# Chunk attention and cosine router: the weight copies at a change of expert move from ScalarE to GpSimd

## The chip, the cores and the metric

The kernel runs on one core of one Trainium2 chip. The metric is device time in microseconds of one execution; where several runs are shown, their median. The profile is of one execution, taken by the hardware profiler, and has its own time.

## The reference

Attention in chunks of 64 rows feeds a mixture of experts in which each token goes to one expert of eight.

```python
# attention, B = 8, H = 8, S = 576, D = 64, in chunks of 64 rows
scores = scale * np.matmul(q_c, k_c.transpose(0, 1, 2, 4, 3))
attn = softmax(scores)
out = np.matmul(attn, v_c)              # x = out as (4608, 512)
# router and experts, E = 8, w1 (8, 512, 1024), w2 (8, 1024, 512)
expert_idx = np.argmax(logits, axis=1)
for e in range(E):
    mask = expert_idx == e
    h = np.maximum(x[mask] @ w1[e], 0.0)
    out[mask] = gate_w[mask, None] * (h @ w2[e])
```
All data are float32.

## The kernel before

The first part, up to about 180 us, computes the attention and the router and scatters the token rows, ordered by expert, into a DRAM buffer. The second part, with which this document deals, goes through these rows in steps. A step j takes 128 token rows in two halves of 64, s = 0 and s = 1; each half belongs to one expert, half 0 going up through the experts from the first, half 1 coming down from the last. Each half has its own weights in SBUF: `w1_sb[s]`, `w2_sb[s]` in two buffers, and `next_w1[s]`, into which the w1 of the half's next expert is loaded well ahead (`load_behind`, L177).

From step 3 on, `hidden_fast` computes the hidden layer with seven block products in place of eight (Strassen's method). The w1 of a half is cut in four blocks B11, B12, B21, B22; four combinations T1 to T4 of them are made by VectorE in `add_up` (L291), T1, T2 and T4 into `sums`, T3 in the place of B12. The inputs have combinations S of their own (`add_x`, L318, four VectorE instructions of 128x128 with both inputs in SBUF). On TensorE the products (L342) come in the order p1 (B11), p2 (B21), p3 (B22), p5 (T1), p6 (T2), p7 (T3), p4 (T4), 16 matmuls each with both halves in turn, in six PSUM banks used round and round; so p4 has the bank of the same step's p1. Behind p4 stands `result` of the step before: 64 matmuls with w2 (L413) into one of two PSUM tiles.

The order on every engine is written out by hand (`manual_schedule`), so each engine's queue follows the source:

- ScalarE, in `hidden_fast`: the copy U of p1 out of PSUM (L377), square root and exponent for the gates (L224, L231, each with a table load), relu of c11, c12 and c22 (L361), then `swap_next`, then relu of the last block, then the scaling y of the finished result (L421).
- VectorE: c11 = U + p2, `turn_xb` and `add_x` for the next step (L203, L318), the sums for c12 and c22 (L374), then `swap_next`, the last block U - p4 (L374), and two transposes into hT (L368).
- GpSimd: one indirect DMA per step that scatters y to the output (L428). It waits for y.
- SyncE: the loads of rows, of w2 and of `next_w1`.

`swap_next` calls `take_next`. For each half it reads one number of `swap` into a register of the engines named (L137) and branches on it (L299, "tc.If"). If the half's expert changes, three quarters of w1 are copied from `next_w1` to `w1_sb` (L301), 1024 elements on each of 128 partitions per copy, and `add_up` makes T1 to T4 from `next_w1` (four VectorE instructions). If not, the engine adds to its semaphore what the skipped instructions would have added, and goes on. The next step's p1, p2 and p3 wait for these copies' semaphore in either case.

```python
p1 = product(x[:, 0, 0], "B11")
nc.scalar.copy(U, p1)
...
relu(1, 1, c22)
p4 = product(x[:, 1, 1], "T4")
swap_next()
add(U, U, p4, ALU.subtract)
relu(1, 0, U)
```

Of the kernel before, what the change touches and what calls it, by code (L numbers as in the profile page):

```python
# [16 lines left out]
ENG = mybir.EngineType  # L17
# [8 lines left out]
def kernel(  # L26
# [11 lines left out]
    nc = tc.nc  # L38
# [69 lines left out]
    swap = keep.tile([P, NST], I32, name="swap")  # L108
# [3 lines left out]
    def of_step(s, j):  # L112
        c = NST - 1 - (j - NE)
        return slice(G * s, G * s + 1), slice(c, c + 1)
# [21 lines left out]
    def number(ap, top, *engines):  # L136
        return nc.values_load(  # L137
            ap,
            engines=engines,
            min_val=0,  # L140
            max_val=top,
            skip_runtime_bounds_check_because="a count of comparisons, less than this",
        )
# [132 lines left out]
    def block(s, m, w1=None):  # L276

        if m in TS:
            return sums_sb[s][:, TS.index(m)]
        u, v = UV[m]  # L280
        return (w1 or w1_sb)[s].rearrange("p (u c) (v x) -> p u v c x", u=2, v=2)[:, u, v]

    def add_up(s, w1, which):
        for o, a, b in (
            ("T1", "B12", "B11"),
            ("T2", "B22", "T1"),
            ("T3", "B22", "B12"),
            ("T4", "T2", "B21"),
        ):
            if o in which:  # L290
                nc.vector.tensor_tensor(  # L291
                    block(s, o), block(s, a, w1), block(s, b, w1), ALU.subtract
                )

    def take_next(j):

        for s in range(2):
            f = number(swap[of_step(s, j)], 1, ENG.DVE, ENG.Activation)
            with tc.If(f > 0):  # L299
                for m in ("B11", "B21", "B22"):  # L300
                    nc.scalar.copy(block(s, m), block(s, m, next_w1))  # L301
                add_up(s, next_w1, ("T1", "T2", "T3", "T4"))

    def quarters(xT):
# [808 lines left out]
    next_w1 = [late_p.tile([P, KD, F], FP32, name=f"next_w1_{s}") for s in range(2)]  # L1113
# [6 lines left out]
    with (  # L1120
# [18 lines left out]
        for j in range(LEAST - 1):  # L1139
# [9 lines left out]
            def swap_next():  # L1149
                if NE <= n < LEAST:  # L1150
                    take_next(n)
# [93 lines left out]
```

## Time and profile before

| what | value |
|---|---|
| three runs | median 676.58 us (675.12 to 679.66) |
| the profiled execution | 675.66 us |
| its span | 673.8 us |
| mean granted TensorE clock | 0.988 |
| ScalarE, L301 copies | 18, mean 1044 ns |
| VectorE, L291 subtractions at a change | 24, mean 1218 to 1226 ns |
| VectorE, L318 | 132, mean 292 ns |
| GpSimd, L428 scatters of whole rows | 36, mean 1002 ns |
| loads of swap (L137) on ScalarE | 64, median 453 ns |
| loads of swap on VectorE | 64, median 524 ns |

The span runs from the first to the last instruction of the program on the core; what lies around it is start and end of the execution. In the views, a row of a group has the line, the engine, the operation, the tiles out<-in and the shape, then busy time and mean duration, then the engine's idle time ahead of it and what ended that. In the timeline a row begins with its start and duration in us, and ends with the idle time ahead of it and its releaser. PEld is TensorE's weight load, and a q after an engine's name is its sequencer.

### The profile page before, as it was taken

To read this page: it belongs to the slowest core of one execution; us is meant where nothing else is said; L and a number is where in the kernel's file an instruction comes from. 1 tells how busy PE (TensorE), PEld (TensorE's weight loads), DVE (VectorE), ACT (ScalarE), POOL (GpSimd) and SP (SyncE) were. 2 spreads that over 40 slices of the span, in tenths; PEclk is the share of its full clock that TensorE was granted. 3 is DMA by queue.
4 is the path that set the end of the run, shared out by engine and by line. 5 is a ranking of instruction groups with operands and counts; after the bars stand their busy time and mean duration, and the time that the engine had idled before them with its cause. 6 is when DMAs were issued, how large, how long until landed. Compare 5 with 4: busy or idle time off the path is not lost. (4 is left out here: it accounts for less than half of the span.)

```text
span 673.8 us, 24854 instructions
## 1 busy us (share of the span) xinstructions
PE 628.7 (93%) x9744; PEld 366.8 (54%) x9744; DVE 420.9 (62%) x1140; ACT 445.8 (66%) x776; POOL 158.4 (24%) x237
## 2 busy tenths in 40 slices
PE   5989999999789999999999999999999999999993
PEld 4867777776446667667434444334444444444441
DVE  3848888887469555656575466767654666564430
ACT  4746667666124777677877867778777777877650
POOL 6738887743311000000100100001001000100101
PEclk9979999999989999999999999999999999999998
DMA  9998899989918711112777111776821114411101
GB/s 249 235 246 235 240 293 267 266 231 348 363 54 302 279 51 46 43 40 71 293 262 282 57 37 48 281 281 228 330 70 44 44 48 162 172 43 34 51 28 37
DMA packets 94686, 112.66 MB, mean 167 GB/s; under 512 B 52460, under 2 KB 72684, under 8 KB 94552
## 3 DMA queue, kind: packets, MB, share of 16 engines
q1 hardware_dynamic: 82824, 72.84, 33.8%
q0 software_dynamic: 11696, 38.04, 17.1%
q8 instruction: 81, 1.33, 0.8%
q14 instruction: 53, 0.43, 0.2%
q10 hardware_dynamic: 32, 0.02, 0.0%
HBM read 334.71 MB, written 22.69 MB: 530 GB/s over the span
## 5 line engine op out<-in xcount | busy, mean ns | idle before, releaser
L413 PE MATMUL y_ps<-w,hT 128*32 128x512 f32 (+1 forms) x2368 | 272.6, 589 | 0.0
L361 ACT ACTIVATE h<-C 64x256 f32<-64x256 f32 x264 | 178.6, 677 | 95.5 <-DVE C L374 68.9
L413 PEld LDWEIGHTS y_ps<-w,hT 128*32 128x32 f32 x2368 | 103.3, 110 | 142.3 <-issue 110.2
L428 POOL DMA_INDIRECT out_dram<-y,spot x36 | 36.1, 1002 | 436.9 <-ACT y L421 208.8
L374 DVE TENSOR_TENSOR C<-C,h 128x256 f32<-128x256 f32 x231 | 96.1, 416 | 49.2 <-DVEq L299 42.5
L342 PE MATMUL h<-w,S 128*32 128x256 f32 x1056 | 95.6, 379 | 0.0
L342 PE MATMUL h<-sums,xbT 128*32 128x256 f32 x1056 | 94.8, 379 | 0.0
L342 PE MATMUL h<-w,xbT 128*32 128x256 f32 x1056 | 78.5, 380 | 7.1 <-ACTq L299 6.0
L368 DVE STREAM_TRANSPOSE hT<-h 128x512 f32<-128x512 f32 x66 | 46.7, 708 | 44.1 <-ACT h L361 44.0
L342 PEld LDWEIGHTS h<-w,xbT 128*32 128x32 f32 x1056 | 43.0, 110 | 39.8 <-ACTq L299 13.4
L342 PEld LDWEIGHTS h<-w,S 128*32 128x32 f32 x1056 | 50.4, 110 | 20.3 <-ACT w L301 0.4
L342 PEld LDWEIGHTS h<-sums,xbT 128*32 128x32 f32 x1056 | 50.0, 110 | 20.3 <-ACT C L377 0.6
L227 DVE TENSOR_SCALAR rn<-rn 128x1 f32<-128x1 f32 x37 | 5.7, 153 | 68.9 <-ACT rn L224 68.9
L342 PE MATMUL h<-sums,S 128*32 128x256 f32 x528 | 47.8, 379 | 0.0
L813 POOL DMA_INDIRECT spots<-xr,dest x36 | 37.4, 1039 | 30.3 <-DVE dest L778 9.0
L203 DVE STREAM_TRANSPOSE xbT<-xin 128x256 f32<-128x256 f32 x73 | 44.2, 643 | 0.5 <-DVE hT L368 0.5
L224 ACT ACT_TABLE_LOAD x34 | 43.6, 1283 | 0.9 <-issue 0.3
L231 ACT ACT_TABLE_LOAD x34 | 43.6, 1283 | 0.6
L421 ACT ACTIVATE y<-y_ps,gate 128x512 f32<-128x512 f32 (+1 forms) x37 | 25.2, 682 | 24.1 <-issue 8.8
L695 ACT COPY xT<-tr 128x512 f32<-128x512 f32 x36 | 21.1, 586 | 29.8 <-PE tr L693 25.4
L585 POOL DMA_DIRECT2D kx<-in_k_dram x36 | 32.0, 891 | 19.7 <-PE tr L608 18.8
L585 POOL DMA_DIRECT2D qx<-in_q_dram x40 | 34.5, 866 | 1.6 <-PE tr L608 0.8
(202 smaller groups left out, 807.9 us busy)
## 6 DMA issues: line engine op xcount, KB each, us to landing
w<-in_moe_w_dram SPq DMA_DIRECT2D x74, 2048.0 KB
next_w<-in_moe_w_dram SPq DMA_DIRECT2D x67, 2048.0 KB
xin<-spots SPq DMA_DIRECT2D x158, 64.0 KB
qx<-in_q_dram POOLq DMA_DIRECT2D x32, 256.0 KB
v<-in_v_dram SPq DMA_DIRECT2D x56, 144.0 KB
kx<-in_k_dram POOLq DMA_DIRECT2D x28, 256.0 KB
spots<-blank SPq DMA_DIRECT2D x9, 144.0 KB
spot<-spots SPq DMA_DIRECT2D x80, 4.0 KB
```

The lines of the kernel that those rows point to most:

```text
L203: nc.vector.transpose(xT[:, :, cols].rearrange("p c (b i) -> p b c i", i=Q), t[:, s * (D // 2) : (s + 1) * (D // 2)].rearrange("p (b i c) ...
L224: nc.scalar.activation(rn, spot[:, j % SPOTS, SQ : SQ + 1], AF.Sqrt)
L231: nc.scalar.activation(sh, sh, AF.Exp, accum_out=gate)
L342: nc.tensor.matmul(ps[t0 : t0 + Q], lhsT=a[:, c, s], rhs=w[:, r], start=c == 0, stop=c == KD // 2 - 1,)
L361: nc.scalar.activation(h[b][G * v : G * v + G, s].rearrange("p (k i) -> p k i", i=Q), x[G * s : G * s + G].rearrange("p (i k) -> p k i", i=Q),
L368: nc.vector.transpose(hT.rearrange("p k (s b i) -> p b s k i", b=2, i=Q)[:, b], h[b].rearrange("p s (k i) -> p s k i", i=Q),)
L374: nc.vector.tensor_tensor(out, a, b, op)
L413: nc.tensor.matmul(ps[Q * r : Q * r + Q, 0:w], lhsT=d["hT"][:, c, Q * t0 : Q * t0 + Q], rhs=w2_sb[s][buf_of(j)][:, c, d0 : d0 + w], start= ...
L421: nc.scalar.activation(y[:, 0:w], ps[:, 0:w], AF.Copy, scale=gate_of.pop(j))
L428: ins = nc.gpsimd.indirect_dma_start(out=to, out_offset=bass.IndirectOffsetOnAxis(ap=at, axis=0), in_=y[:, 0:w], in_offset=None, bounds_ch ...
L585: eng.dma_start(out=x[done : done + n], in_=src[b, :, s : s + n, :].rearrange("h p d -> p h d"),)
L813: ins = nc.gpsimd.indirect_dma_start(out=spots, out_offset=bass.IndirectOffsetOnAxis(ap=at, axis=0), in_=m, in_offset=None, bounds_check=S ...
```

## The change

In `take_next`, GpSimd in place of ScalarE reads `swap`, branches on it, and makes the three copies. ScalarE has no conditional left in these steps. The instructions of TensorE and VectorE are the same in number and order. On GpSimd the two tests and the copies stand between the scatter of one result and the scatter of the next.

```diff
     def take_next(j):
 
         for s in range(2):
-            f = number(swap[of_step(s, j)], 1, ENG.DVE, ENG.Activation)
+            f = number(swap[of_step(s, j)], 1, ENG.DVE, ENG.Pool)
             with tc.If(f > 0):
                 for m in ("B11", "B21", "B22"):
-                    nc.scalar.copy(block(s, m), block(s, m, next_w1))
+                    nc.gpsimd.tensor_copy(block(s, m), block(s, m, next_w1))
                 add_up(s, next_w1, ("T1", "T2", "T3", "T4"))
```

## The prediction

> **What bounds the kernel now.** I read the page's busy times first, then what the matmuls wait for from 250 us to the end (the waits view of PE), then the groups by form of ACT and POOL, and last the timeline around an expert change.
>
> ```profile
> PE 628.7 (93%) x9744; PEld 366.8 (54%) x9744; DVE 420.9 (62%) x1140; ACT 445.8 (66%) x776; POOL 158.4 (24%) x237
> ```
> ```profile
> PE h L342 <- ACTq L299: 6.0, 7, 1.3
> PE h L342 <- ACT w L301: 0.9, 1, 0.9
> ```
> TensorE is the bound, and in the stage concerned the matmuls wait for nothing but ScalarE's conditional (L299 is the If; "ACTq" is ScalarE's sequencer) and its copies. So the change touches the only thing TensorE waits for there. How much that is worth is read from the step starts. I call T the start of a step's first product p1 (B11). In the PE timeline undisturbed steps are 12.91 us apart (302.26 to 315.17). Three stretches are longer: T goes from 302.26 to 370.52 in 5 steps (3.71 us too long), from 409.25 to 492.88 in 6 (6.17) and from 544.51 to 584.14 in 3 (0.90). **10.8 us** in all, more than the 6.9 us of the waits view because an undisturbed p1 overlaps the product before it by 0.57 us. These stretches hold the expert changes: the source view of L301 has 18 copies, three to a half, so six changes; the 64 tests of L299 on ScalarE have 58 skips, which agrees. From the timeline they lie in the steps with T = 302.26 (half 1), 329.67 (half 0), 409.25 (half 0), 422.16 (half 1), 451.83 (half 0), 544.51 (half 0).
>
> ```profile
> 302.26 2.08 PE L342 MATMUL h<-w,xbT 128*32 128x256 f32 x31
> 303.80 0.37 ACT L377 COPY C<-h 128x256 f32<-128x256 f32 x1 [0.18 <-PE h L342]
> 303.89 0.98 POOL L428 DMA_INDIRECT out_dram<-y,spot  x1 [11.93 <-ACT y L421]
> ...
> 307.88 0.29 DVE L318 TENSOR_TENSOR S<-xbT 128x128 f32<-128x128 f32 x1
> ...
> 313.13 1.22 DVE L291 TENSOR_TENSOR sums<-next_w 128x1024 f32<-128x1024 f32 x1 [1.70 <-issue]
> 313.88 2.94 ACT L301 COPY w<-next_w 128x1024 f32<-128x1024 f32 x3 [0.69 <-ACTq L299]
> ...
> 316.67 1.22 DVE L291 TENSOR_TENSOR sums<-sums,next_w 128x1024 f32<-128x1024 f32 x1
> ...
> 317.80 0.41 DVE L374 TENSOR_TENSOR C<-C,h 128x256 f32<-128x256 f32 x1
> ...
> 318.25 1.38 ACT L361 ACTIVATE h<-C 64x256 f32<-64x256 f32 x2 [1.43 <-DVE C L374]
> ...
> 320.24 0.36 ACT L377 COPY C<-h 128x256 f32<-128x256 f32 x1
> ...
> 320.61 0.98 POOL L428 DMA_INDIRECT out_dram<-y,spot  x1 [15.74 <-ACT C L377]
> 320.65 0.66 PEld L342 LDWEIGHTS h<-sums,xbT 128*32 128x32 f32 x16 [0.21 <-ACT C L377]
> ...
> 329.37 0.42 DVE L374 TENSOR_TENSOR C<-C,h 128x256 f32<-128x256 f32 x1 [1.51 <-DVEq L299]
> 329.67 2.46 PE L342 MATMUL h<-w,xbT 128*32 128x256 f32 x30 [1.02 <-ACTq L299]
> ...
> 330.45 1.36 ACT L361 ACTIVATE h<-C 64x256 f32<-64x256 f32 x2 [0.88 <-DVE hT L368]
> ```
> Three things are to be seen. The next p1 (329.67) waits for ScalarE's skipped conditional, which runs late because of the change one step earlier. At the change itself ScalarE is not the last: after its copies (end 316.82) it idles 1.43 us until VectorE has done its four subtractions L291 and the last C. At the other kind of change the same row, at 424.16, idles 0.97. And the last product p4 has a second gate: it reuses p1's PSUM bank and waits for ScalarE's copy U (L377; 0.21 at 320.65).
>
> **What the Trainium skill says.** "SBUF — State Buffer", section "Who interferes with whom": a VectorE instruction with two SBUF inputs contends with a GpSimd instruction that reads SBUF, and whichever is second blocks for the whole instruction. No line of the trace before shows the pair overlapping. "GPSIMD Engine Reference", section 4.1: one-input elementwise work is roughly at line rate; section 3.1 has 1.03 cycles an element for light bodies, 1.8 for a tight loop and 2.6 for two inputs, at 1.2 GHz. The trace leans to the fast end:
>
> ```profile
> L301 ACT COPY w<-next_w 128x1024 f32<-128x1024 f32 x18 | 17.6, 1044 | 1.5 <-ACTq L299 1.4
> ```
> ```profile
> L517 POOL CAST io<-io_i 128x41 f32<-128x41 int32 x1 | 0.2, 225 | 0.0
> L518 POOL CAST at<-part_i 128x1 f32<-128x1 int32 x1 | 0.2, 194 | 0.0
> ```
> 40 elements more cost 31 ns, so 1024 elements are estimated at 0.19 + 1023 x 0.78 ns = 1.0 us. I take 1.0. The ends are the page's 1.03 and 2.6 cycles: 0.9 and 2.2 us, both estimates.
>
> **The change part by part.** ScalarE loses, per step, two loads of swap (0.45 us each) with their branches, and 3 copies at a change (2.94 us from first to last). PE's, VectorE's and SP's instructions stay. GpSimd gains the same two tests and the copies, behind the scatter of the previous result (L428) and ahead of its own step's scatter. That queue has room: POOL idles 436.9 us before the L428 rows.
>
> (a) *The wait of p1.* It becomes a wait for GpSimd. Write u for the start of the U copy; everything on ScalarE and VectorE follows it at fixed distances. The scatter starts at u + 0.09 in a punctual step (303.89 against 303.80), u + 0.37 in a late one (320.61 against 320.24), and takes 0.98. GpSimd's loads take 0.50 and 0.30 (its two at 650 us, the first of which runs beside a scatter), so half 0's copies can start as the scatter ends, u + 1.1 or u + 1.4, and half 1's some 0.25 later. With 1.0 us and 0.05 between, all three are over by u + 4.2 to u + 4.8. They may: p1 to p3, whose weights they overwrite, end by T + 2.6, about u + 1.1, and next_w1 was ordered steps before. The next p1 comes at T + 12.91, which is u + 11.4, or u + 7.8 in the latest step. So p1's 10.8 us go, and with a test skipped nothing is near. This cover fails only when B11 of half 1 comes later than u + 7.
>
> (b) *The wait of p4 stays, and grows.* p4 stands at T + 5.18 (307.44 for T = 302.26); it needs u + 0.42 (320.65 against 320.24). Call the lateness L = u - (T + 1.54). p4 is stopped from L = 3.2; some 0.35 is caught up in the matmuls after it (at T = 435.81 p4 came 0.92 late and the next products of y ended 0.54 late), so a step is lengthened by L - 3.6. What makes L is the loop from one U copy to the next. In a step without change it is 12.19 now (320.24 to 332.43). After: the last C ends at 329.79, relu follows 0.03 later instead of at 330.45, so it is 12.19 - 0.62 = 11.57. At a change it is 16.44 (half 1 at T = 302.26), 16.25 (half 1 at 422.16), 15.34 (half 0). VectorE sets these, so they keep their length. L changes per step by the loop minus 12.91, minus the lengthening: up by 3.53, 3.34 or 2.43 at a change, down by 1.34 otherwise.
>
> (c) *The new contention c.* VectorE's four L318 subtractions and additions (two SBUF inputs) want to start at u + 4.08 (307.88), and everything after them on VectorE up to the loop's end is behind them. If they wait for the copy then running: copies over at u + 4.2 (punctual half 0), 4.5 (punctual half 1), 4.6 (late half 0), 4.8 (late half 1) give c = 0.2, 0.5, 0.5, 0.7 us. From below c is 0 (no lock); a gain is excluded, since a copy can't speed L318 up. From above the two alternate or the copy is slow, see the rivals. I take the values named. The L291 subtractions start at u + 7.9 or later, when the copies are done.
>
> The sum, one L per step: after the change at 302.26, L = 3.53 + 0.5 = 4.03, lengthens 0.43; down to 3.60 - 1.34 = 2.26; second change, 2.26 + 2.43 + 0.5 = 5.19, lengthens 1.59; then it decays. At 409.25: 2.43 + 0.2 = 2.63, nothing; at 422.16: 2.63 + 3.34 + 0.7 = 6.67, lengthens 3.07; 2.26; at 451.83: 5.19, lengthens 1.59. At 544.51: 2.63, nothing. Together 6.7 us. So 10.8 us go, 6.7 come back at p4: **4.1 us less**. The profiled execution took 675.66 us around a span of 673.8; it becomes 671.6. It stands 0.9 below the median of 676.58 of the runs shown, so the median becomes **672.5**.
>
> **Rivals.** *No contention* (c = 0). For it: nothing in the trace shows a lock. The same sum gives 0 + 1.02 + 2.17 + 1.09 = 4.3 us at p4, 6.5 less, 670.1.
> *The whole 10.8 us*: the loop at a change was ScalarE's after all. It gives 665.8. Against it stand the 1.43 and 0.97 us ScalarE idles there.
> *Slower: GpSimd's copies take long.* At 2 us a copy they last until u + 7.7, and the L318 instructions get in only between them or after them: c up to 3.4 us. In the sum each 1 us of c at all six changes costs 6 us; the bill passes 10.8 us at c = 1.3. With three copies from u + 1.4 that is a copy of 1.3 us or more. With c = 3.4 it is 23.5 us at p4, 12.7 more than now, 689. With c = 1.9 it is 14.5, and 680.3. For it: the page's 1.8 and 2.6 cycles, and that two consecutive copies may take the lock in turn with four short L318. Against: the CAST rows.
> *The copies don't come early*, because GpSimd is held by its scatter or by a late next_w1: they'd be where ScalarE had them, c moves from L318 to L291 and p1 still waits; about today's time, 676. Against: u + 1.4 above. I count it with the slower ones.
>
> **How the numbers follow.** Forecast with contention of 0.1 to 1.0 us: 0.47, with 670.5 to 675.5. No contention: 0.22. The whole 10.8: 0.06. Slow copies, alternation or late copies: 0.25, half of it above 683. The middle 8 in 10 reach from the best no-contention values, with the runs' own spread, to the middle of the slow case: 668.5 to 681. A change of 1% is 6.8 us, about what a measurement of this kernel can tell from none. Faster by more than that: the whole-gain case and half of the no-contention one, 0.17; slower: half of the slow case, 0.12; within: 0.71.
>
> **What would show it.** Waits of PE on L299 and L301 gone from the stage; in their place PEld or PE waits of h on ACT C (L377), about 7 us in four steps, the largest in the step after 422.16. GpSimd copies near 1.0 us, starting 1.1 to 1.7 us after U. L318 pushed by 0.2 to 0.7 us at the six changes and nowhere else. U-to-U loops of 11.6 us in steps without change and unchanged, plus c, in those with one. It is wrong if copies take over 1.3 us, if p1 waits for POOL, or if the loop at a change shrinks.

## The result, and the profile after

Over 21 runs of each kernel on one chip the median is 672.30 us after (667.78 to 675.39) and 674.52 us before (670.35 to 679.66). The ratio is 0.9953, with a 95% interval of 0.9934 to 0.9973: a gain of 1.8 to 4.5 us, under 1%. The forecast was 672.5 us and a gain of 4.1 us. The medians themselves lie 2.2 us apart. That the level agrees within 0.2 us is luck: before itself ran 2.1 us lower here than in the three runs the forecast started from, and the gain came out smaller by about as much.

The profiled execution after took 673.40 us around a span of 671.6 us, 2.2 us less span than before. I measure the expert stage by one figure throughout: the **excess**, which is the time from the fifth U copy (after: at 264.88 us) to that of the last full step (after: at 635.16 us), less 28 undisturbed steps of 12.91 us. Before it is 10.8 us, after it is 8.8 us. So the stage gives 2.0 of the 2.2 us of span. The forecast excess was 6.7 us: p4's lengthenings. The excess leaves out what comes ahead of the fifth U copy, which starts at 261.93 to 273.56 us in the profiles of this document; the times of whole executions contain that too.

The page's first row after:

```profile
PE 626.3 (93%) x9744; PEld 343.6 (51%) x9744; DVE 425.9 (63%) x1140; ACT 427.7 (64%) x758; POOL 175.2 (26%) x255
```

ACT has 18 instructions and 18.1 us less and POOL 18 instructions more, as the diff says. VectorE has the same instructions, but is busy 5.0 us longer: the first sign of where the gain is lost.

The waits of PE from 250 us to the end (engine, tile and line, then who released it: us in total, times, the longest):

```profile
PE h L342 <- DVEq L299: 2.6, 2, 1.8
PE h L342 <- ACT C L377: 2.3, 4, 1.3
PE h L342 <- DVE C L374: 1.5, 1, 1.5
```

The waits for ScalarE's conditional and for its copies are gone. In their place stand the late U (L377), as forecast for p4, and two waits for VectorE that the forecast didn't list: p5 for VectorE's second test (its T1 is one of the conditional's sums), and p7 for the reader of its PSUM bank. These two come in front of p4 in late steps, and take a part of the same lateness. The timeline of PE shows both in the worst case, the step with T = 434.23:

```profile
434.23 1.91 PE L342 MATMUL h<-w,xbT 128*32 128x256 f32 x32
...
440.30 1.07 PE L342 MATMUL h<-w,S 128*32 128x256 f32 x16 [1.54 <-DVE C L374]
442.67 1.07 PE L342 MATMUL h<-sums,xbT 128*32 128x256 f32 x16 [1.30 <-ACT C L377]
```

p7 stands 1.54 us, then p4 1.30 us more. The whole step is 3.28 us too long.

The same change as the one shown of before (half 1, here T = 302.07), in the timeline without PE:

```profile
303.70 0.98 POOL L428 DMA_INDIRECT out_dram<-y,spot  x1 [11.93 <-ACT y L421]
304.45 1.35 SPq L177 DMA_DIRECT2D next_w<-in_moe_w_dram  x2
...
305.92 1.09 DVE L229 TENSOR_SCALAR sh<-spot,lmax,rn 128x8 f32<-128x8 f32 x1
305.94 2.99 POOL L301 COPY w<-next_w 128x1024 f32<-128x1024 f32 x3 [1.27 <-DVE rn L228]
...
306.92 0.41 DVE L374 TENSOR_TENSOR C<-C,h 128x256 f32<-128x256 f32 x1
...
308.54 0.54 DVE L318 TENSOR_TENSOR S<-xbT 128x128 f32<-128x128 f32 x1
...
309.12 0.29 DVE L318 TENSOR_TENSOR xbT<-xbT 128x128 f32<-128x128 f32 x1
```

Three things are to be seen. The copies take 1.0 us each, as forecast, but begin 2.33 us after U (U starts at 303.61), not 1.35 to 1.65. The scatter ended at 304.68, so it isn't what they waited for. And two VectorE instructions are stretched while a copy runs: L318 from 0.29 to 0.54, which was forecast as a class, and ahead of it L229, eight columns wide, from 0.29 to 1.09, which was not priced at all. L229 ends at 307.01, 0.03 us after the first copy, although its record begins 0.02 us ahead of the copy's.

The loop from U to the next U at each change gives the contention c, as the difference to the loops of before. Times in us; the copies' start is counted from U:

| change at U | half | loop before | loop after | c | c forecast | copies start | L229 | first L318 |
|---|---|---|---|---|---|---|---|---|
| 303.61 | 1 | 16.44 | 17.40 | 0.96 | 0.5 | 2.33 | 1.09 | 0.54 |
| 332.56 | 0 | 15.35 | 16.04 | 0.69 | 0.5 | 1.93 | 0.69 | 0.52 |
| 409.61 | 0 | 15.34 | 15.87 | 0.53 | 0.2 | 1.77 | 0.52 | 0.54 |
| 425.48 | 1 | 16.25 | 16.78 | 0.53 | 0.7 | 1.76 | 0.53 | 0.52 |
| 453.80 | 0 | 15.32 | 17.10 | 1.78 | 0.5 | 1.34 | 2.08 | 0.29 |
| 544.82 | 0 | 15.34 | 15.89 | 0.55 | 0.2 | 1.78 | 0.53 | 0.55 |

The shortest loops of late steps without a change are 11.54 to 11.58 us, where 11.57 was forecast and 12.19 measured before.

The fifth change is the costly one. Its timeline:

```profile
455.14 3.00 POOL L301 COPY w<-next_w 128x1024 f32<-128x1024 f32 x3
...
456.11 2.08 DVE L229 TENSOR_SCALAR sh<-spot,lmax,rn 128x8 f32<-128x8 f32 x1
...
458.10 0.41 DVE L374 TENSOR_TENSOR C<-C,h 128x256 f32<-128x256 f32 x1
```

L229 arrives as the first copy is ending, and stays until 458.19, when the third has ended (458.14): it sat out two copies. Everything behind it on VectorE is 1.8 us later.

### The profile page after: what moved, and what is told of

It reads as the page before. It is cut to its first block, busy times and chain, and to the rows that moved or that the text cites. A ratio compares the mean times of both kernels' runs of the same rounds, so it can differ in the third digit from the quotient of the medians.

```text
span 671.6 us, 24878 instructions
## 1 busy us (share of the span) xinstructions
PE 626.3 (93%) x9744; PEld 343.6 (51%) x9744; DVE 425.9 (63%) x1140; ACT 427.7 (64%) x758; POOL 175.2 (26%) x255
## 5 line engine op out<-in xcount | busy, mean ns | idle before, releaser
L413 PE MATMUL y_ps<-w,hT 128*32 128x512 f32 (+1 forms) x2368 | 265.4, 591 | 3.6 <-DMA w<-in_moe_w_dram 3.6
L413 PEld LDWEIGHTS y_ps<-w,hT 128*32 128x32 f32 x2368 | 84.1, 111 | 160.0 <-issue 147.6
L374 DVE TENSOR_TENSOR C<-C,h 128x256 f32<-128x256 f32 x231 | 96.1, 416 | 49.8 <-DVEq L299 39.2
L342 PE MATMUL h<-sums,xbT 128*32 128x256 f32 x1056 | 81.0, 380 | 5.0 <-DVEq L299 2.6
L342 PE MATMUL h<-w,S 128*32 128x256 f32 x1056 | 81.4, 379 | 3.2 <-DVE w L291 1.7
L342 PE MATMUL h<-w,xbT 128*32 128x256 f32 x1056 | 68.5, 379 | 0.0
L342 PEld LDWEIGHTS h<-w,xbT 128*32 128x32 f32 x1056 | 37.7, 110 | 34.1 <-issue 17.0
L342 PEld LDWEIGHTS h<-sums,xbT 128*32 128x32 f32 x1056 | 38.5, 110 | 28.8 <-ACT C L377 4.3
L342 PEld LDWEIGHTS h<-w,S 128*32 128x32 f32 x1056 | 39.1, 110 | 26.0 <-DVE C L374 2.0
L203 DVE STREAM_TRANSPOSE xbT<-xin 128x256 f32<-128x256 f32 x73 | 44.5, 649 | 0.5 <-DVE hT L368 0.5
L342 PE MATMUL h<-sums,S 128*32 128x256 f32 x528 | 40.9, 379 | 0.0
```

Source lines behind the costliest of these rows:

```text
L203: nc.vector.transpose(xT[:, :, cols].rearrange("p c (b i) -> p b c i", i=Q), t[:, s * (D // 2) : (s + 1) * (D // 2)].rearrange("p (b i c) ...
L342: nc.tensor.matmul(ps[t0 : t0 + Q], lhsT=a[:, c, s], rhs=w[:, r], start=c == 0, stop=c == KD // 2 - 1,)
L374: nc.vector.tensor_tensor(out, a, b, op)
L413: nc.tensor.matmul(ps[Q * r : Q * r + Q, 0:w], lhsT=d["hT"][:, c, Q * t0 : Q * t0 + Q], rhs=w2_sb[s][buf_of(j)][:, c, d0 : d0 + w], start= ...
```

## The experiments

The theory, from these rows: after's remaining excess is two things. 4.3 us is the stop of p4 behind VectorE's four subtractions L291, which the forecast has without contention. The rest is contention, nearly all of it on L229 and the first L318. The rival is that something else in moving the conditional costs the 4.5 us (the two tests on GpSimd, the scatter's queue, the writes into w1). The kernels below tell these apart, and then ask what would take either part away. Each ratio is to before on the same chip.

**One column.** GpSimd copies one column of each block; the other 1023 elements of a partition are left out.

```diff
-nc.gpsimd.tensor_copy(block(s, m), block(s, m, next_w1))
+to, src = block(s, m), block(s, m, next_w1)
+nc.gpsimd.tensor_copy(to[:, 0, 0:1], src[:, 0, 0:1])
```

> GpSimd keeps its tests and waits, but at a change it copies one column of each block and leaves out the other 1023 elements. Theory (GpSimd's copies hold VectorE up, L229 and L318, and p4 then waits for U): L229 and L318 keep their 0.29 us, the loops at a change go back to 16.4, 16.3 and 15.3 us, and with L = 3.53, 4.30, 5.77, 4.30 against a free 3.2 the step excess over 12.91 us falls from 9.2 us in the changed kernel to about 5.0 us, 4 us faster than it. Rival (VectorE is held by something else that came with the change, such as semaphores or the tests on GpSimd): the loops stay at 15.9 to 17.4 us and the excess at about 9 us.

671.74 us against 681.3, ratio 0.9886 (0.9836 to 0.9936). The excess is 4.3 us, in three lengthenings of 1.04, 2.19 and 1.06 us, within 0.03 us each of the forecast's rival without contention. The loops at a change are back at 15.31 to 16.47 us. In the groups by form of VectorE:

```profile
L229 DVE TENSOR_SCALAR sh<-spot,lmax,rn 128x8 f32<-128x8 f32 x29 | 8.4, 291 | 1.0
```

After the change the same group has a mean of 419 ns. The tests and the order of the queue are unchanged here, so they aren't the cause: the copies' length is. By these two profiles contention costs 4.5 us of the excess.

**Fill.** Is it the copies' reads or their writes? One column is copied, then the three blocks are filled with zeros by GpSimd; the weights are left out.

```diff
+to, src = block(s, "B11"), block(s, "B11", next_w1)
+nc.gpsimd.tensor_copy(to[:, 0, 0:1], src[:, 0, 0:1])
 for m in ("B11", "B21", "B22"):
-    nc.gpsimd.tensor_copy(block(s, m), block(s, m, next_w1))
+    nc.gpsimd.memset(block(s, m), 0.0)
```

> At a change GpSimd copies one column, so that it starts when the copies did, and then fills the three blocks with zeros in place of copying, so it writes as much as before and reads nothing. Theory A (only GpSimd's reads contend, with whatever VectorE reads second): L229 and L318 both keep 0.29 us, excess about 5.0 us as with one column. Theory B (L229, one tensor of 8 columns, contends as an operation that uses both of VectorE's ports, writes too; L318 by its second input alone): L229 is stretched to the end of a fill, by 0.2 to 0.9 us, L318 is not; excess 6 to 8 us. Rival (writes alone contend): both are stretched as with the copies, excess about 9 us.

674.17 us against 681.3, ratio 0.9899 (0.9865 to 0.9934); excess 4.7 us. On the time this is as with one column. The timeline of the last change (L320 is L318 here, L376 is L374):

```profile
545.26 2.75 POOL L303 MEMSET w<- 128x1024 f32 x3
...
545.55 1.58 DVE L229 TENSOR_SCALAR sh<-spot,lmax,rn 128x8 f32<-128x8 f32 x1
545.75 1.38 DVE L376 TENSOR_TENSOR C<-C,h 128x256 f32<-128x256 f32 x1
546.08 1.22 DVE L203 STREAM_TRANSPOSE xbT<-xin 128x256 f32<-128x256 f32 x2
547.33 0.29 DVE L320 TENSOR_TENSOR S<-xbT 128x128 f32<-128x128 f32 x1
547.66 0.29 DVE L320 TENSOR_TENSOR xbT<-xbT 128x128 f32<-128x128 f32 x1
```

The two-input L320 beside a running fill keeps its 0.29 us. L229's record is stretched by the fill too (to 0.68, 1.01 and 1.58 us, in the three of six changes where the two overlap). Here the record of L376 behind it is stretched as well, from 0.41 to 1.38 us, and both end at 547.13. Yet the transposes L203 go on meanwhile, and L320 starts 4.1 us after U as without any contention. ScalarE's reader of L229's result waits 0.73 us in this change, with room to spare: the loops at the changes are within 0.13 us of those before. So the expectation's theory B had the records right and theory A the time: a write beside L229 ends it late but doesn't hold up VectorE, and what costs time is the copies' reads.

**Sums later.** If p4's stop is VectorE's four L291 in front of the last C, they can stand behind it. GpSimd's copies move in the source with them, but GpSimd's own queue keeps its order.

```diff
 p4 = product(x[:, 1, 1], "T4")
-swap_next()
 add(U, U, p4, ALU.subtract)
 relu(1, 0, U)
+swap_next()
```

> VectorE makes the new T1 to T4 after the last block U - p4 in place of before it; all else is as in the changed kernel. Theory (VectorE's four subtractions ahead of U - p4 set the loop at a change): relu and U are no longer late, the loop at a change falls from 15.9 to 17.4 us to about 12.9 us, PE's waits for ACT C (L377) all but vanish, excess 0 to 1.5 us in place of 9.2, so 8 to 9 us faster than the changed kernel and 1.5% faster than before. Rival (the loop at a change is set on ScalarE, or TensorE has another gate right behind, such as T1 for p5 or hT for the product with w2): excess stays above 5 us.

670.59 us against 681.3, ratio 0.9858 (0.9803 to 0.9914). The excess is 0.8 us. The only wait of PE on these lines from 250 us to the end:

```profile
PE h L342 <- DVEq L299: 0.6, 1, 0.6
```

The timeline of the first change:

```profile
311.97 1.10 DVE L229 TENSOR_SCALAR sh<-spot,lmax,rn 128x8 f32<-128x8 f32 x1
312.01 3.00 POOL L301 COPY w<-next_w 128x1024 f32<-128x1024 f32 x3 [1.27 <-DVE rn L228]
...
317.41 4.14 ACT L361 ACTIVATE h<-C 64x256 f32<-64x256 f32 x6 [2.59 <-DVE C L374]
...
320.13 1.23 DVE L291 TENSOR_TENSOR sums<-next_w 128x1024 f32<-128x1024 f32 x1 [1.19 <-DVEq L299]
...
322.57 0.37 ACT L377 COPY C<-h 128x256 f32<-128x256 f32 x1 [0.17 <-PE h L342]
```

At this change the contention is all there (L229 at 1.10), but U waits for PE again, not for VectorE: the loop at this change is 12.90 us. The subtractions run after the relus. The two costs don't add: contention costs only where it meets a loop that is already longer than TensorE's step.

**Test on ScalarE too.** What was it on ScalarE that delayed the relu in steps without change: reading and testing the number, or what follows? After, with ScalarE named as a third engine that reads and branches, and does nothing in the branch.

```diff
-f = number(swap[of_step(s, j)], 1, ENG.DVE, ENG.Pool)
+f = number(swap[of_step(s, j)], 1, ENG.DVE, ENG.Pool, ENG.Activation)
```

> As the changed kernel, but ScalarE also reads swap and branches, with nothing to do in the branch. The copies stay on GpSimd and p1 waits for GpSimd alone. Theory (freeing ScalarE of the tests only shortens the loop in steps without a change, 12.2 to 11.56 us; what freed p1 is where the copies' semaphore is raised): p1 still doesn't wait, the loop without a change is 12.2 us again, lateness decays by 0.7 in place of 1.35 a step, excess 10 to 11 us in place of 9.2, 1 to 1.5 us slower than the changed kernel. Rival (ScalarE's tests themselves held p1): p1 waits again after each change, excess over 12 us.

679.62 us against 681.3, ratio 0.9971 (0.9942 to 1.0000). The loop without change stays at 11.55 to 11.59 us, where 12.2 was expected: my expectation of it was wrong. The source view of L299:

```profile
L299 POOLq COMPARE_BRANCH  x70: 38/45/55, 217.8 to 627.5; - x70
L299 DVEq COMPARE_BRANCH  x70: 47/56/72, 224.9 to 635.5; - x70
L299 ACTq COMPARE_BRANCH  x70: 38/45/50, 225.3 to 635.2; - x70
L299 POOLq EVENT_SEMAPHORE  x58: 17/17/17, 218.0 to 627.7; - x58
L299 DVEq EVENT_SEMAPHORE  x58: 21/21/21, 225.2 to 635.7; - x58
```

ScalarE branches 70 times, but with nothing of its own to skip it raises no semaphore. Before, the same view has 58 of ScalarE, the first 1.2 us after its branch. The order of the queue shows the rest. Before, in the step ahead of the first change, the relu ends at 300.26 us, the first raise of the skipped copies' semaphore comes at 300.29, and only then the second test's load of 0.45 us, its branch and its raise; the next relu starts at 301.13. Here, in the same step, both tests are done at 303.40, while the relu still runs to 303.86. So it was the raise, which came only after the relu ahead of it and kept the second test behind it, that cost the 0.6 us, not the test as such. The excess of 9.2 us isn't comparable in full: in this profile the granted clock averaged 0.77 over 10 us inside one of the lengthened stretches (a stretch's busy times, then the clock, the DMA share and GB/s). That step was lengthened by 6.2 us, where the changed kernel's was by 3.3.

```profile
448.00:458.00 10.00, 10.00 (x88) 2.79 (x84) 7.12 (x21) 7.42 (x13) 0.00 (x0) 0.77 0.63 245
```

**The change again,** unedited, on another chip, with the kernels that follow.

> The changed kernel once more, on the chip of the following three, so that they are compared with it and with before there. Theory: excess of the steps over 12.91 us 9 to 10 us as before, ratio to the kernel before 0.994 to 0.998; L229 stretched at all six changes, p1 never waiting. Rival (the first profile's excess was a chance of that execution): another sum, under 7 us.

670.39 us against 675.36, ratio 0.9917 (0.9886 to 0.9948); excess 7.8 us. L229 took 1.10, 0.57, 0.52, 0.54, 1.12 and 0.53 us: the one at the fifth change took 1.12 here and 2.08 above. The same code thus meets the copies differently in two executions. Both the excess and the ratio missed the expected 9 to 10 us and 0.994 to 0.998. Two profiles of one kernel differ by 1.0 us of excess, so a difference of that size between single profiles of two kernels shows nothing.

**ScalarE with the sums later.** How much of the gain of sums later needs GpSimd? Before, with `swap_next` moved by one line.

```diff
 p4 = product(x[:, 1, 1], "T4")
-swap_next()
 add(U, U, p4, ALU.subtract)
+swap_next()
 relu(1, 0, U)
```

> The kernel before, copies on ScalarE, with only VectorE's new sums moved behind the last block. Theory (with the sums out of the way ScalarE's copies are the next to set the loop, so the change of engine is needed for the gain that the later sums give): loop at a change about 15.0 us, ScalarE's end of copies at u + 12.4 to 13.0 plus 2; p1 still waits for ScalarE's copies or tests; excess 6 to 9 us, ratio to before 0.993 to 0.998. Rival (the later sums alone do it, whichever engine copies): loops near 12.9 us, excess under 2 us, ratio about 0.986.

669.90 us against 675.36, ratio 0.9917 (0.9887 to 0.9948); excess 6.3 us. PE's wait, and the timeline of ScalarE at the first change:

```profile
PE h L342 <- ACTq L299: 3.7, 4, 1.3
```
```profile
310.73 2.94 ACT L301 COPY w<-next_w 128x1024 f32<-128x1024 f32 x3 [0.70 <-ACTq L299]
313.58 1.38 ACT L361 ACTIVATE h<-C 64x256 f32<-64x256 f32 x2
...
315.57 0.36 ACT L377 COPY C<-h 128x256 f32<-128x256 f32 x1
```

With VectorE out of the way ScalarE's own copies stand in front of the relu and of U. From before's 10.8 us the excess falls by 4.5 with the order alone, by 2.0 with the engine alone (3.0 in the change again), and by 10.0 with both (0.8; there the sums stand one line later still, behind the relu): each hides a part of the other. On the time, the order alone and the engine alone have the same ratio on this chip, 0.9917.

**w1's loads first.** Why do the copies start late? In the SyncE queue the conditional load of `next_w1` stands behind that of w2. If a semaphore that the copies wait for rises only when SyncE has passed that load, taken or not, its place sets their start. The timeline after, at the third change:

```profile
408.62 1.35 SPq L177 DMA_DIRECT2D w<-in_moe_w_dram  x2
...
409.70 0.97 POOL L428 DMA_INDIRECT out_dram<-y,spot  x1 [11.93 <-ACT y L421]
...
411.17 1.57 SPq L177 DMA_DIRECT2D next_w<-in_moe_w_dram  x2
...
411.38 3.00 POOL L301 COPY w<-next_w 128x1024 f32<-128x1024 f32 x3 [0.70 <-PE h L342]
```

GpSimd idles 0.70 us after its scatter, until 0.21 us after SyncE's next load is issued. The first, second and last change show the same distance, 0.20 to 0.22 us. At the fourth the copies follow GpSimd's own second test, 0.40 us after the scatter, and at the fifth the scatter itself. The test is to put `load_behind` ahead of `load_w2`.

```diff
 result(j, ps_y)
-if NE <= next_of(j) < NJ:
-    load_w2(next_of(j))
 if NE - 1 <= n < LEAST - 1:
     load_behind(n)
...
+if NE <= next_of(j) < NJ:
+    load_w2(next_of(j))
```

> The changed kernel with SyncE's conditional load of next_w1 put ahead of the one of w2 in each step. Theory (GpSimd's first copy at a punctual change is held until SyncE has passed the previous step's load of next_w1, at T + 2.8 for half 0 and T + 3.7 for half 1, taken or not): copies at punctual changes start at u + 1.1 to 1.4 in place of u + 1.8 to 2.3; they still run over L229 at u + 2.3, which waits 0.5 to 0.9 us, and are over before L318 at u + 4.1, which keeps 0.29; excess 8 to 10 us, no gain. Rival (the copies wait for p1 or for GpSimd's own tests): starts stay at u + 1.8 and u + 2.3.

675.30 us against 675.36, ratio 0.9996 (0.9975 to 1.0017). The timeline of the same change:

```profile
409.86 1.36 SPq L177 DMA_DIRECT2D next_w<-in_moe_w_dram  x2
...
411.22 0.37 ACT L377 COPY C<-h 128x256 f32<-128x256 f32 x1 [0.18 <-PE h L342]
...
412.27 2.03 POOL L301 COPY w<-next_w 128x1024 f32<-128x1024 f32 x2
...
413.52 1.79 DVE L229 TENSOR_SCALAR sh<-spot,lmax,rn 128x8 f32<-128x8 f32 x1
```

The copies now start the moment the scatter ends, 1.05 us after U, here and at the last change: that was the forecast's start, and the load's place is what delayed them there. At the first and the fourth change they start 1.51 and 1.76 us after U, behind the second test; at the second and the fifth, in late steps, they still start some 0.2 us after SyncE's load. L229, expected to wait 0.5 to 0.9 us, meets the second copy, and sits out the second and the third (1.79 us here and at the last change). The excess is 8.4 us, against 7.8 in the change again. An earlier start, on which the forecast's small c rested, is no cure. The kernel is 4.9 us slower than the change again, of which the excess shows 0.6. The fifth U copy comes 2.2 us later (267.63 us against 265.45), but it moves by several us among the other kernels too; whether that comes from the new order the runs don't show.

**Quarter copies.** If an instruction waits for the copy then running, shorter copies cost it less. Each copy is cut in four of 256 columns.

```diff
+for c in range(2):
+    for x in (slice(0, 256), slice(256, 512)):
+        nc.gpsimd.tensor_copy(to[:, c, x], src[:, c, x])
```

> The changed kernel with each copy made in four of 256 columns, the same bytes. Theory (VectorE is blocked to the end of the one GpSimd instruction that is running, so shorter ones block less): copies of 0.35 to 0.45 us each, L229 and the L318 wait at most one of them each, c 0.1 to 0.5 us in place of 0.5 to 1.8, excess 6 to 8 us. Rival 1 (they take turns): each of the L318 is stretched, c over 1 us, excess over 10. Rival 2 (bandwidth is shared, it's no lock): the stretch is the same as with whole copies.

670.56 us against 675.36, ratio 0.9928 (0.9902 to 0.9954). The timeline of the first change (L304 are the copies, L321 is L318):

```profile
306.32 4.39 POOL L304 COPY w<-next_w 128x256 f32<-128x256 f32 x12 [1.25 <-DVE rn L228]
306.33 0.41 DVE L229 TENSOR_SCALAR sh<-spot,lmax,rn 128x8 f32<-128x8 f32 x1
...
308.61 0.37 DVE L321 TENSOR_TENSOR xbT<-xbT 128x128 f32<-128x128 f32 x1
```

L229 is at most 0.53 us at any change, and L318 takes 0.30 to 0.40. c is 0.26 to 0.52 us at each change, never above after's, as the length of the copy that runs would have it. The excess is 6.3 us, 1.5 less than in the change again on this chip. The time doesn't show it: 670.56 us against the change again's 670.39.

**Sums later again,** on that last chip.

> The changed kernel with VectorE's new sums behind the last block, once more, beside the next one on one chip. Theory: excess of the steps 0 to 1.5 us, ratio to the kernel before 0.982 to 0.989, so the changed kernel's 0.9917 to 0.9953 is beaten. Rival (its first ratio was a chance): 0.991 or more.

666.34 us against 675.04, ratio 0.9865 (0.9822 to 0.9908); excess 1.2 us. It repeats, and is the fastest version found. The copies of the fifth change came late here and in its first run, 6.45 and 7.27 us after U, and p1 waited for GpSimd in neither.

**Sums later with quarter copies.**

> As the one before it, with the copies in quarters. Theory (with the sums behind the last block VectorE has slack at a change, so what GpSimd's copies hold up there is hidden): the same time within 0.3%, excess 0 to 1.5 us. Rival (the rest of the excess is contention): excess falls to nothing, 1 us faster.

671.73 us against 675.04, ratio 0.9949 (0.9911 to 0.9986); excess 7.3 us. The expectation missed. PE's wait, and the timeline of the worst change (no other kernel here has this wait):

```profile
PE h L345 <- POOLq L299: 5.2, 2, 4.3
```
```profile
454.11 8.14 POOL L304 COPY w<-next_w 128x256 f32<-128x256 f32 x12 [6.96 <-DMA next_w<-in_moe_w_dram]
454.56 1.37 DVE L291 TENSOR_TENSOR sums<-next_w 128x1024 f32<-128x1024 f32 x1 [0.30 <-issue]
...
457.18 1.41 DVE L291 TENSOR_TENSOR w<-next_w 128x1024 f32<-128x1024 f32 x1
...
457.42 0.60 PE L345 MATMUL h<-w,xbT 128*32 128x256 f32 x4
```

`next_w1` landed late here, for a reason the run doesn't show, so the copies began 8.03 us after U, beside VectorE's L291. Four of the twelve took 1.39 us in place of 0.40, as many as there are L291, and all twelve took 8.14 us where the first change of quarter copies has 4.39. p1 waited 4.3 us for GpSimd. Right after that wait the granted clock was low as well, which made the products of this step some 1.7 us longer than those of the step before (the clock is the third figure from the end):

```profile
460.00:470.00 10.00, 7.64 (x110) 4.34 (x114) 4.89 (x14) 4.72 (x8) 3.25 (x8) 0.83 0.68 228
```

This is the forecast's case of copies that don't come early. At the same change of sums later, three whole copies that began 7.27 us after U met two of the L291; one of them took 2.04 us, and all three 3.99. Whether whole copies that begin as late as these would have lost less isn't shown.

## Why the prediction was right, and what was off

**(a) p1's wait goes: right.** No PE wait on L299 of ACT or on L301 is left, and p1 waits for nothing of GpSimd. The copy was forecast at 1.0 us; the source view of L301 has (minimum/median/maximum in ns):

```profile
L301 POOL COPY w<-next_w x18: 1030/1038/1052, 305.9 to 548.6; 128x1024 f32<-128x1024 f32 x18
```

So the trace agrees with the Trainium skill, "GPSIMD Engine Reference", section 4.1, that one-input elementwise work runs near line rate. The slow-copy rival, which needed 1.3 us, falls on this number. One reason given for the early start failed: "next_w1 was ordered steps before" is true of the data, but the copies began some 0.2 us after SyncE had issued the previous step's conditional load, later than the scatter, in four of six changes. At the fourth change GpSimd's second test stood between, 0.40 us where 0.25 was forecast. p1 had 4 us and more to spare (p1 of the step at T = 434.23 needed copies that had ended at 430.24), so it cost nothing there; w1's loads first shows the mechanism at two of the changes.

**(b) p4's stop by a late U: right.** The loop without change was forecast at 11.57 us and is 11.54 to 11.58 at its shortest. Put the measured loops, of the six changes and 11.55 between them, into the prediction's own sum, and it gives 0.89 + 1.77 + 3.23 + 2.83 = 8.7 us, where the trace has 0.90, 1.78, 3.28 and 2.83, 8.8 in all. That p5 and p7 take a part of it ahead of p4 doesn't change the sum. One column confirms the same model at c = 0: 4.3 forecast, 4.3 measured.

**(c) The contention: real, but the term is mis-sized.** It was forecast at 0.2 to 0.7 us a change on L318 and came at 0.53 to 1.78, and the lengthenings grew by 0.47, 0.19, 0.21 and 1.24 us over the forecast: 2.1 us, all of the error. The working priced only the two-input instructions. The Trainium skill, "SBUF — State Buffer", section "Who interferes with whom", also names `tensor_scalar` among those that can take the port pair that GpSimd shares, in a mode that depends on their operands, and says that in this mode the one who comes second blocks fully. L229 is a `tensor_scalar`, of eight columns; the prediction skipped it. The traces agree as far as the copies go: L229 is stretched at all six changes after, to 0.52 us at least, and nowhere with one column. Whether L229 runs in that mode they don't show, and beside the fill VectorE didn't block fully: the instructions behind L229 went on. Nor do they show which of L229's accesses meets the copy. They also agree that a two-input instruction isn't held by a GpSimd instruction that only writes (0.29 us beside the fill).

**The sum.** 4.1 us was forecast. The profile's excess shows 2.0, and the ratio gives 3.2 us (1.8 to 4.5). Both lie below the forecast, which still lies in the upper part of that interval. The profile of one execution can't settle it closer: the change again had an excess of 7.8 us and a ratio of 0.9917 (0.9886 to 0.9948), a larger gain than the first comparison, with intervals that overlap.

**The rivals.** No contention is refuted by one column. The whole 10.8 us is refuted by the loops at a change, which didn't shrink; it is nearly reached by sums later, which takes away VectorE's part as well. That copies don't come early was not the case here, but sums later with quarter copies shows that it happens in this program, and that p1 then waits 4.3 us.

## What to carry to other kernels

When work moves to an idle engine, ask of every instruction that runs beside it, the smallest too, whether the two engines hold each other up; here an eight-column instruction that takes 0.29 us alone made a step's loop up to 1.8 us longer, since all of its engine's work stands behind it. When two engines take turns at being last (ScalarE's copies, VectorE's sums), moving one of them shows little until the other is moved as well: 2.0 to 3.0 and 4.5 us of excess alone, 9.6 to 10.0 together. Before relying on a copy that starts early, follow its semaphore to the last instruction that raises it, skipped ones included.

## What the runs showed of the hardware beyond what was expected

- A VectorE `tensor_scalar` of 128x8 that meets back-to-back GpSimd copies doesn't always get in between two of them: it waited out two in 2.08 and 1.79 us.
- Beside a GpSimd fill the same instruction ended up to 1.3 us late by its record, and all but the one right behind it ran on in time; beside a copy they waited.
- A branch's record on ScalarE is 45 ns long here. Raising the skipped work's semaphore came only after the engine's earlier work, and with the second test behind it cost the relu 0.6 us in a late step.
- GpSimd's copy of 128x1024 float32 took 1.04 us, ScalarE's 1.04 us too; of 128x256 some 0.40 us. Three blocks took 2.99 us whole and 4.39 us in quarters at the first change.
- Where GpSimd's quarter copies met VectorE's L291, both were slowed: the copies took 1.39 us in place of 0.40, the L291 1.30 to 1.41 in place of 1.22.
